# Regrouping the backward attention loop: where a group's sums, transpositions, query gradient and job matmuls stand, and which engines copy and add

## The chip, the cores and the metric

The kernel runs on one core of a Trainium2 chip. Its engines work from queues of their own and meet at semaphores: TensorE (PE, with its weight loads as PEld), VectorE (DVE), ScalarE (ACT), GpSimd (POOL) and SyncE (SP). SP here only issues DMAs, GpSimd issues DMAs and does a little arithmetic. Matmul results go to PSUM, everything else lies in SBUF. The metric is the device time of the one core in microseconds.

## The reference

The program computes a transformer block of attention and a gated feed-forward part that both read the same normalised input, and then the gradients of that sum by an output gradient. There are 2048 tokens, a model width of 448, 16 heads of 28 and a hidden width of 1792.

```
x  = A_x
xn = layernorm(x)
q, k, v = split(xn @ wqkv)                     # 16 heads of 28
p  = softmax(q @ k.T * 28 ** -0.5)
A  = (p @ v) @ wo
B  = (silu(xn @ w_gate) * (xn @ w_up)) @ w_down
out = x + A + B
grads of out by x, wqkv, wo, w_gate, w_up, w_down, for a given grad_out
```

Outputs are out and the six gradients, all in bf16. In the backward pass of attention, p is computed again from q and k. With dp = dO @ v.T (less its row sums), ds = p * dp; then dv = p.T @ dO, dk = ds.T @ q and dq = ds @ k, the last two times the scale.

## The kernel before

The program has three stages. The first (to about 690 us in the profile) normalises, projects, runs the forward attention and, between its steps, the feed-forward part with its weight gradients. The second is the backward attention, from about 694 to 1503 us; the change lies in it alone. The third adds up the gradient of x.

**Units and groups.** The backward loop (line 944) goes over 512 units. A unit is one pair of heads, one block of 512 keys (kc) and one tile of 128 queries (qi within a half w of the sequence). Eight units with the same pair, key block and half are a group, so there are 64 groups; W is the number of the group and pos the place of step k in it (k = 8 W + pos). Two groups cover all 16 query tiles of a key block; eight groups cover a pair.

**A unit.** TensorE computes the scores s of unit k (line 957, two matmuls, one per head, in two row strips of the array) and dp of unit k - 1 (line 967, in the other two strips). ScalarE takes E = exp(s) (line 976). VectorE multiplies dp by E into ds (line 984); ds tiles hold two units. The row sums and the softmax denominators are folded into spare columns of the operands, so that this one product gives ds.

**PSUM.** s, dp and the output of the transpositions share three buffers "sd" of two banks each, taken in turn: the s of a unit normally takes the buffer whose ds product was three units ago, and the dp the buffer of the E just computed. One bank, "aux", is shared by the query gradient and the jobs, one after the other. One bank, "acc", holds the sums for keys and values.

**A group's other work** is placed by hand at positions of the loop, on TensorE in the order of the program:
- acc_mm (line 857): the sums of E times dO and ds times q, four matmuls a unit, in four column strips. Three units at position 3 and five at position 6.
- The query gradient needs ds transposed, tile dsT. Units 0 to 5 of a group are transposed by three DMAs from the SP queue (line 986), each of two units (512 KB). Units 6 and 7 are transposed on TensorE by pe_transpose (line 887) at position 2 of the next group, 16 matmuls against the identity; the two halves are copied out by ScalarE and VectorE (line 895).
- dq_mm (line 897): the query gradient of the group before, 16 matmuls, one half at position 4 and one at position 5. dq_out (line 911): at position 6 VectorE scales the result out of PSUM and adds it to an fp32 tile dq_acc over the four key blocks; at the fourth it writes a bf16 tile, which an SP transposition and two GpSimd DMAs take away one step later.
- A job: a piece of other work that needs TensorE, one for nearly every group (list at lines 729 to 733): 16 rows of the block's output (y, 19 matmuls), 2 x 16 rows of the gradient that comes back through the feed-forward weights (dx, 14 or 15 matmuls), and 14 pieces of the gradient of wqkv (dwq, 64 small matmuls). A job's matmuls are dealt out in thirds over position 7 of the group before and positions 0 and 1; job_out (line 834) at position 2 is ScalarE's copy out of PSUM and a DMA from GpSimd. The job of group W is loaded two groups ahead (job_load, line 735).

**Buffers.** E has eight buffers, ds five of two units, dsT two. The loop runs eight steps past the last unit.

**Order of the queues.** The kernel is scheduled by hand: each engine executes in program order. In a step that is: SP loads; scores; dp; job_out and dq_out; exp; ds; the DMA transposition of ds; DMAs put off from earlier steps (sp_later); job matmuls; pe_transpose; acc_mm; dq_mm.

Of the kernel before, what the change touches and what calls it, by code (L numbers as in the profile page):

```python
# [25 lines left out]
P = 128  # L26
# [3 lines left out]
SCALE = DH ** -0.5  # L30
# [8 lines left out]
def kernel(  # L39
# [19 lines left out]
    pe, act, dve, pool, sp = nc.tensor, nc.scalar, nc.vector, nc.gpsimd, nc.sync  # L59
# [46 lines left out]
    op1 = bst.enter_context(tc.tile_pool(name="op1", bufs=1))  # L106
# [38 lines left out]
    for b in range(1, 4):  # L145
# [9 lines left out]
        out=r_ones[:], in_=ident_f[:].rearrange("p (a b) -> p a b", b=HP)[:, :, 28:30],  # L155
# [529 lines left out]
    ast = ExitStack()  # L685
    ckp = ast.enter_context(tc.tile_pool(name="ckp", bufs=3))
    spg_.append(ast.enter_context(tc.tile_pool(name="spg", bufs=2)))
    ework = ast.enter_context(tc.tile_pool(name="ework", bufs=8))
    dwork = ast.enter_context(tc.tile_pool(name="dwork", bufs=5))
    twin = ast.enter_context(tc.tile_pool(name="twin", bufs=2))  # L690
    dqa = ast.enter_context(tc.tile_pool(name="dqa", bufs=1))
    ps_acc = ast.enter_context(tc.tile_pool(name="ps_acc", bufs=1, space=PSUM))

    UW = 8
# [116 lines left out]
    def job_mms(i, ps):  # L811
        j = jobs[i]
        if j[0] == "dwq6":
            return dwq_half_mms(0, j[1], ps, True, 0) + dwq_half_mms(0, j[1] + 1, ps, False, 192)
        if j[0] == "dwq":
            return dwq_mms(j[1], j[2], ps)
        if j[0] == "y":
            t, x = chunk[i]
            out = []
            for n in range(NFC + G):  # L820
                rhs = (wtile["wd"][:, n, :] if n < NFC else wo_pad[:, n - NFC, :D])
                out.append(lambda n=n, rhs=rhs: pe.matmul(ps[:, :D], lhsT=t[:, n, :], rhs=rhs,  # L822
                                                          start=(n == 0), stop=False))
            out.append(lambda: pe.matmul(ps[:, :D], lhsT=ident_bf[:], rhs=x[:], start=False, stop=True))
            return out
        t, x = chunk[i]
        w = wtile[("wg", "wu")[j[1]]]
        out = [lambda n=n: pe.matmul(ps[:, :D], lhsT=t[:, n, :], rhs=w[:, n, :],  # L828
                                     start=(n == 0), stop=(n == NFC - 1 and x is None)) for n in range(NFC)]
# [57 lines left out]
    def pe_transpose(W):  # L887

        ds, dsT = DS[W * 4 + 3], st[("dsT", W)]
        ps = ps_sd.tile([P, 2, 8, P], BF16, name="sd")  # L890
        for u in range(2):
            for i in range(8):
                pe.transpose(ps[:, u, i, :], ds[:, u, i // 4, (i % 4) * P:(i % 4 + 1) * P], ident_bf[:])  # L893
        for u, eng in enumerate((act.copy, dve.tensor_copy)):
            eng(out=dsT[:, 6 + u].rearrange("p j c q -> p (j c) q"), in_=ps[:, u])  # L895

    def dq_mm(W, half):
        pr, kc, w, _ = units[W * UW]
# [13 lines left out]
    def dq_out(W):  # L912
        pr, kc, w, _ = units[W * UW]
        g, hp = pr // 2, pr % 2
        ps = st["dq"]
        if (pr, w) not in dqacc:
            dqacc[(pr, w)] = dqa.tile([P, 512], FP32, name=f"dq_acc{w}")
        acc = dqacc[(pr, w)]
        if kc == 0:
            dve.tensor_scalar(out=acc[:], in0=ps[:], scalar1=SCALE, scalar2=None, op0=ALU.mult)  # L920
            return
        if kc < 3:
            dve.scalar_tensor_tensor(out=acc[:], in0=ps[:], scalar=SCALE, in1=acc[:], op0=ALU.mult, op1=ALU.add)
            return
        o = outp.tile([P, 512], BF16, name="dq_o")
        dve.scalar_tensor_tensor(out=o[:], in0=ps[:], scalar=SCALE, in1=acc[:], op0=ALU.mult, op1=ALU.add)
        dq = dsp[pr][1]

        def later():
            sp.dma_start_transpose(out=dq[:, w].rearrange("p c s r -> p c (s r)"), in_=o[:])  # L930
            for s_ in range(2):
                k0 = 4 * w + 2 * s_
                pool.dma_start(
                    out=dqkv_d[k0:k0 + 2, 64 * hp:64 * hp + 64, g, :].rearrange("k p s -> p k s"),
                    in_=o[64 * s_:64 * s_ + 64, :].rearrange("p (k s) -> p k s", k=2))
        sp_later.append((k_now[0] + 1, later))
# [4 lines left out]
    job_load(1)  # L941
    job_load(2)
    fillers = []
    for k in range(N + UW):
        W, pos = k // UW, k % UW
        k_now[0] = k
        if k < N:
            pr, kc, w, qi = units[k]
            if pos == 0:
                job_load(W + 2)  # L950
            if pos == 4:
                extra_load(W)
            q, kv = qd[pr]
            qt = 8 * w + qi
            s_ps = ps_sd.tile([P, 2, 512], FP32, name="sd")
            for j in range(2):
                pe.matmul(s_ps[:, j, :], lhsT=q[HP * j:HP * j + HP, qt * P:(qt + 1) * P],  # L957
                          rhs=kv[HP * j:HP * j + HP, kc * 512:(kc + 1) * 512],
                          start=True, stop=True, tile_position=(HP * j, 0))
        if 1 <= k <= N:  # L960
            pr, kc, w, qi = units[k - 1]
            q, kv = qd[pr]
            qt = 8 * w + qi
            d_ps = ps_sd.tile([P, 2, 512], FP32, name="sd")
            for j in range(2):
                r = 64 + HP * j
                pe.matmul(d_ps[:, j, :], lhsT=q[r:r + HP, qt * P:(qt + 1) * P],  # L967
                          rhs=kv[r:r + HP, kc * 512:(kc + 1) * 512],
                          start=True, stop=True, tile_position=(r, 0))
        if pos == 2 and W in jobs:  # L970
            job_out(W, st["job"])
        if pos == 6 and W >= 1:
            dq_out(W - 1)
        if k < N:
            E[k] = ework.tile([P, 2, 512], BF16, name="E")
            act.activation(out=E[k][:], in_=s_ps[:], func=ACT.Exp, scale=SCALE)  # L976
        if 1 <= k <= N:
            u = k - 1
            if qi == 0:
                st[("dsT", u // UW)] = twin.tile([P, UW, 2, 4, P], BF16, name="dsT")  # L980
            if u % 2 == 0:
                DS[u // 2] = dwork.tile([P, 2, 2, 512], BF16, name="ds")
            ds = DS[u // 2]
            dve.tensor_tensor(out=ds[:, u % 2], in0=d_ps[:], in1=E[u][:], op=ALU.mult)  # L984
            if qi in (1, 3, 5):
                sp.dma_start_transpose(
                    out=st[("dsT", u // UW)][:, qi - 1:qi + 1].rearrange("p u j c q -> p (u j c) q"),
                    in_=ds[:].rearrange("p u j c -> p (u j c)"))
        while sp_later and sp_later[0][0] <= k:
            sp_later.pop(0)[1]()  # L990

        if pos == 7 and W + 1 in jobs:
            st["job"] = ps_x.tile([P, 512], FP32, name="aux")
            fillers = job_mms(W + 1, st["job"])
        if pos in (7, 0, 1):
            n = -(-len(fillers) // (3 - (pos + 1) % UW))
            for f in fillers[:n]:
                f()
            fillers = fillers[n:]
        if pos == 2 and W >= 1:  # L1000
            pe_transpose(W - 1)
        if pos == 3:
            for u in range(max(k - 6, 0), k - 3):
                acc_mm(u)
        if pos in (4, 5) and W >= 1:
            dq_mm(W - 1, pos - 4)
        if pos == 6:
            for u in range(k - 6, min(k - 1, N)):
                acc_mm(u)
    while sp_later:  # L1010
        sp_later.pop(0)[1]()
    ast.close()
# [110 lines left out]
```

## Time and profile before

| | us |
|---|---|
| Median of 3 runs (lowest, highest) | 1583.67 (1571.13, 1587.04) |
| The profiled execution | 1572.41 |
| Its span, first to last instruction | 1570.6 |
| TensorE busy, matmuls | 1447.8 |
| VectorE busy | 1123.3 |
| ScalarE busy | 1171.0 |
| GpSimd busy | 231.4 |
| First and last ds product of the backward loop | 694.2, 1503.0 |
| First matmul of the last stage | 1516.4 |

The profile is one execution. Its page gives the busy time of each engine, the span in 40 slices, the chain of work that ended last, and the costliest groups of instructions by source line, with what ended the idle time before them. The trace behind it can be asked for the waits between engines, for a timeline of one engine in a stretch of time, and for busy times and the granted TensorE clock of a stretch. In timeline rows the columns are start, length, engine, line, operation, tile written and tiles read, shapes, count, and in square brackets the idle time before and what ended it. A busy engine need not be at its peak: matmuls overlap, and four that lie in different strips of the array run side by side.

### The profile page before, as it was taken

To read this page: it belongs to the slowest core of one execution; us is meant where nothing else is said; L and a number is where in the kernel's file an instruction comes from. 1 tells how busy PE (TensorE), PEld (TensorE's weight loads), DVE (VectorE), ACT (ScalarE), POOL (GpSimd) and SP (SyncE) were. 2 spreads that over 40 slices of the span, in tenths; PEclk is the share of its full clock that TensorE was granted. 3 is DMA by queue.
4 is the path that set the end of the run, shared out by engine and by line. 5 is a ranking of instruction groups with operands and counts; after the bars stand their busy time and mean duration, and the time that the engine had idled before them with its cause. 6 is when DMAs were issued, how large, how long until landed. Compare 5 with 4: busy or idle time off the path is not lost.

```text
span 1570.6 us, 31535 instructions
## 1 busy us (share of the span) xinstructions
PE 1447.8 (92%) x12278; PEld 592.2 (38%) x12278; DVE 1123.3 (72%) x1459; ACT 1171.0 (75%) x1312; POOL 231.4 (15%) x431
## 2 busy tenths in 40 slices
PE   6889999999999999969989999899899899998968
PEld 3233333333333333323333344333335334533424
DVE  7465656665666666538878888788888888998835
ACT  4578888888888877637767777677777788887824
POOL 4001111111111111110111111101102111110212
PEclk7799999999999999979999999999999999999979
DMA  5566647776767778579999999999999999999974
GB/s 160 114 147 139 145 102 162 144 150 127 157 140 154 139 152 171 129 189 210 227 219 232 220 164 201 202 206 222 205 185 202 210 229 193 198 204 202 166 221 134
DMA packets 764854, 277.69 MB, mean 177 GB/s; under 512 B 730960, under 2 KB 744208, under 8 KB 764704
## 3 DMA queue, kind: packets, MB, share of 16 engines
q1 hardware_dynamic: 748944, 238.90, 77.9%
q0 software_dynamic: 14960, 36.60, 8.5%
q8 instruction: 96, 1.57, 0.4%
q14 instruction: 54, 0.44, 0.1%
q10 hardware_dynamic: 800, 0.17, 0.1%
HBM read 64.15 MB, written 59.24 MB: 79 GB/s over the span
## 4 chain that ended last, share of the span: by engine, by line
PE 72%; DMA 11%; DVE 7%; ACT 6%; issue 2%; SPq 1%; DVEq 0%; ACTq 0%; POOL 0%
PE s_ps L651 9%; PE f_ps L413 8%; DMA dsT<-ds 8%; PE f_ps L439 8%; PE sd L957 7%; PE aux L828 6%; PE acc L867 5%; PE o_ps L628 5%; PE aux L822 4%; PE aux L908 3%; PE sd L967 3%; PE f_ps L198 3%; ACT E L976 3%; ACT dsT L895 3%; PE sd L1039 2%; PE sd L893 2%
## 5 line engine op out<-in xcount | busy, mean ns | idle before, releaser
L984 DVE TENSOR_TENSOR ds<-sd,E 128x1024 bf16<-128x1024 f32 x512 | 610.5, 1219 | 91.7 <-PE sd L967 40.6
L976 ACT ACTIVATE E<-sd 128x1024 bf16<-128x1024 f32 x512 | 522.4, 1027 | 202.1 <-PE sd L967 142.8
L655 ACT ACTIVATE eT<-s_ps 128x1024 bf16<-128x1024 f32 x512 | 496.5, 1021 | 137.7 <-PE s_ps L651 136.7
L957 PE MATMUL sd<-KV,QD 32*128 32x512 bf16 x1024 | 203.7, 392 | 37.1 <-DVE dsT L895 18.7
L967 PE MATMUL sd<-KV,QD 32*128 32x512 bf16 x1024 | 204.9, 391 | 9.5 <-ACT E L976 7.5
L651 PE MATMUL s_ps<-qT,kT 32*128 32x512 bf16 x1024 | 196.9, 392 | 0.5 <-ACT eT L655 0.5
L957 PEld LDWEIGHTS <-QD 32*128 32x128 bf16 x1024 | 61.0, 91 | 216.1 <-issue 204.5
L867 PE MATMUL acc<-E,dOsp 128*32 128x512 bf16 x1024 | 141.5, 400 | 0.2 <-DMA ck<-hO_d 0.2
L867 PE MATMUL acc<-ds,Qsp 128*32 128x512 bf16 x1024 | 141.5, 401 | 0.0
L439 PE MATMUL f_ps<-xnT,wgu 128*128 128x512 bf16 x448 | 119.3, 384 | 9.0 <-DVE w_sb L465 9.0
L908 PE MATMUL aux<-dsT,Ksp 128*32 128x512 bf16 x1024 | 92.7, 402 | 28.3 <-DMA dsT<-ds 28.2
L651 PEld LDWEIGHTS <-kT 32*128 32x128 bf16 x1024 | 47.4, 91 | 162.0 <-issue 158.2
L628 PE MATMUL o_ps<-eT,v_sp 128*32 128x512 bf16 x1024 | 104.0, 399 | 4.3 <-DMA v_sp<-vT 4.1
L828 PE MATMUL aux<-W,ck 128*128 128x448 bf16 x448 | 101.6, 355 | 0.0
L413 PE MATMUL f_ps<-xn_sp,f_sp 128*128 128x448 bf16 x448 | 98.9, 354 | 0.0
L967 PEld LDWEIGHTS <-QD 32*128 32x128 bf16 x1024 | 76.9, 91 | 58.5 <-issue 45.0
L413 PEld LDWEIGHTS <-f_sp 128*128 128x128 bf16 x672 | 58.9, 98 | 66.9 <-issue 20.4
L895 DVE COPY dsT<-sd 128x1024 bf16<-128x1024 bf16 x64 | 44.2, 691 | 50.9 <-ACT dsT L895 50.9
L893 PE MATMUL sd<-ident_bf,ds 128*128 128x128 bf16 x1024 | 69.3, 221 | 2.5 <-DVE ds L984 1.7
L451 DVE SCALAR_TENSOR_TENSOR g<-t_sb,f_ps 128x512 f32<-128x512 f32 x56 | 38.4, 685 | 44.0 <-ACT t_sb L449 44.0
L895 ACT COPY dsT<-sd 128x1024 bf16<-128x1024 bf16 x64 | 64.9, 1014 | 6.5 <-PE sd L893 3.9
L893 PEld LDWEIGHTS <-ds 128*128 128x128 bf16 x1024 | 59.2, 99 | 17.3 <-issue 14.5
(145 smaller groups left out, 1695.5 us busy)
## 6 DMA issues: line engine op xcount, KB each, us to landing
ck<-hO_d SPq DMA_DIRECT2D x17, 576.0 KB, 4.8
hO_d<-hduT SPq DMA_DIRECT2D x56, 128.0 KB, 3.4
da_d<-hduT SPq DMA_DIRECT2D x56, 128.0 KB, 3.0
du_d<-hduT SPq DMA_DIRECT2D x56, 128.0 KB, 3.3
ck<-da_d SPq DMA_DIRECT2D x16, 448.0 KB, 4.2
ck<-du_d SPq DMA_DIRECT2D x16, 448.0 KB, 4.1
dq_c<-dqkv_d SPq DMA_DIRECT2D x8, 768.0 KB, 5.4
dqkv_d<-dkv_o POOLq DMA_DIRECT2D x64, 64.0 KB, 4.5
```

The costliest lines, as they stand in the source:

```text
L413: pe.matmul(acc[:, :D], lhsT=src[:, t, wi, :], rhs=rhs[:, t, :D], start=(t == 0), stop=(t == NT - 1))
L439: pe.matmul(st[name][:], lhsT=w(c), rhs=src[:, tsl, c, :], start=(c == 0), stop=(c == 3))
L628: pe.matmul(o_ps[HP * hh:HP * (hh + 1), :], lhsT=v[:, kt, HP * hh:HP * (hh + 1)], rhs=e[hh // 2][:, hh % 2, :], start=(kt == 0), stop=(kt ...
L651: pe.matmul(s_ps[:, j, :], lhsT=kT[r:r + HP, kt * P:(kt + 1) * P], rhs=qT[r:r + HP, qc * 512:(qc + 1) * 512], start=True, stop=True, tile_ ...
L655: act.activation(out=e[:], in_=s_ps[:], func=ACT.Exp, scale=SCALE)
L828: out = [lambda n=n: pe.matmul(ps[:, :D], lhsT=t[:, n, :], rhs=w[:, n, :], start=(n == 0), stop=(n == NFC - 1 and x is None)) for n in ran ...
L867: pe.matmul(acc[r:r + HP, :], lhsT=src[:, qt, 64 * hp + HP * j:64 * hp + HP * j + HP], rhs=m[:, j, :], start=(qt == 0), stop=(qt == NT - 1 ...
L893: pe.transpose(ps[:, u, i, :], ds[:, u, i // 4, (i % 4) * P:(i % 4 + 1) * P], ident_bf[:])
L957: pe.matmul(s_ps[:, j, :], lhsT=q[HP * j:HP * j + HP, qt * P:(qt + 1) * P], rhs=kv[HP * j:HP * j + HP, kc * 512:(kc + 1) * 512], start=Tru ...
L967: pe.matmul(d_ps[:, j, :], lhsT=q[r:r + HP, qt * P:(qt + 1) * P], rhs=kv[r:r + HP, kc * 512:(kc + 1) * 512], start=True, stop=True, tile_p ...
L976: act.activation(out=E[k][:], in_=s_ps[:], func=ACT.Exp, scale=SCALE)
L984: dve.tensor_tensor(out=ds[:, u % 2], in0=d_ps[:], in1=E[u][:], op=ALU.mult)
```

## The change

The group's work gets other positions, and two steps other engines.

- The sums: five units of the group before at position 0, the other three at position 3.
- pe_transpose of the group before at position 1 (was 2), and both copies out of PSUM by VectorE.
- The query gradient, both halves at position 2, of the group two back (was: of the group before, at 4 and 5). Its dq_out is at position 3.
- dq_out: ScalarE scales the result out of PSUM into fp32, and GpSimd adds it to dq_acc; the bf16 result comes from GpSimd's add too. A new pool dqs has two buffers for that.
- A job's matmuls are dealt out over positions 3 to 7 of its own group; job_out is at position 0 of the next.
- The DMA transposition of ds, and the claim of the dsT buffer with it, stand at the end of a step, after TensorE's work.
- E gets nine buffers. The loop runs twelve steps past the last unit, for the query gradients of the last two groups.

```diff
-    ework = ast.enter_context(tc.tile_pool(name="ework", bufs=8))
+    ework = ast.enter_context(tc.tile_pool(name="ework", bufs=9))
+    dqs = ast.enter_context(tc.tile_pool(name="dqs", bufs=2))
...
-        for u, eng in enumerate((act.copy, dve.tensor_copy)):
-            eng(out=dsT[:, 6 + u].rearrange("p j c q -> p (j c) q"), in_=ps[:, u])
+        for u in range(2):
+            dve.tensor_copy(out=dsT[:, 6 + u].rearrange("p j c q -> p (j c) q"), in_=ps[:, u])
...
+        d = acc if kc == 0 else dqs.tile([P, 512], FP32, name="dq_s")
+        act.activation(out=d[:], in_=ps[:], func=ACT.Copy, scale=SCALE)
         if kc == 0:
-            dve.tensor_scalar(out=acc[:], in0=ps[:], scalar1=SCALE, scalar2=None, op0=ALU.mult)
             return
         if kc < 3:
-            dve.scalar_tensor_tensor(out=acc[:], in0=ps[:], scalar=SCALE, in1=acc[:], op0=ALU.mult, op1=ALU.add)
+            pool.tensor_tensor(out=acc[:], in0=acc[:], in1=d[:], op=ALU.add)
             return
         o = outp.tile([P, 512], BF16, name="dq_o")
-        dve.scalar_tensor_tensor(out=o[:], in0=ps[:], scalar=SCALE, in1=acc[:], op0=ALU.mult, op1=ALU.add)
+        pool.tensor_tensor(out=o[:], in0=acc[:], in1=d[:], op=ALU.add)
...
-    for k in range(N + UW):
+    for k in range(N + UW + 4):
...
-        if pos == 2 and W in jobs:
-            job_out(W, st["job"])
-        if pos == 6 and W >= 1:
-            dq_out(W - 1)
+        if pos == 0 and W - 1 in jobs:
+            job_out(W - 1, st["job"])
+        if pos == 3 and W >= 2:
+            dq_out(W - 2)
...
+        if pos == 0 and 1 <= W <= NW:
+            for u in range(k - 8, k - 3):
+                acc_mm(u)
+        if pos == 1 and 1 <= W <= NW:
+            pe_transpose(W - 1)
+        if pos == 2 and W >= 2:
+            dq_mm(W - 2, 0)
+            dq_mm(W - 2, 1)
+        if pos == 3 and 1 <= W <= NW:
+            for u in range(k - 6, k - 3):
+                acc_mm(u)
+        if pos == 3 and W in jobs:
             st["job"] = ps_x.tile([P, 512], FP32, name="aux")
-            fillers = job_mms(W + 1, st["job"])
-        if pos in (7, 0, 1):
-            n = -(-len(fillers) // (3 - (pos + 1) % UW))
+            fillers = job_mms(W, st["job"])
+        if pos >= 3:
+            n = -(-len(fillers) // (8 - pos))
...
-        if pos == 2 and W >= 1:
-            pe_transpose(W - 1)
-        if pos == 3:
-            for u in range(max(k - 6, 0), k - 3):
-                acc_mm(u)
-        if pos in (4, 5) and W >= 1:
-            dq_mm(W - 1, pos - 4)
-        if pos == 6:
-            for u in range(k - 6, min(k - 1, N)):
-                acc_mm(u)
+        if 1 <= k <= N and qi in (1, 3, 5):
+            Wd = (k - 1) // UW
+            if qi == 1:
+                st[("dsT", Wd)] = twin.tile([P, UW, 2, 4, P], BF16, name="dsT")
+            sp.dma_start_transpose(
+                out=st[("dsT", Wd)][:, qi - 1:qi + 1].rearrange("p u j c q -> p (u j c) q"),
+                in_=ds[:].rearrange("p u j c -> p (u j c)"))
```

More of the change, by code (lines that the diff above doesn't have):

```diff
@@ L978 @@
             u = k - 1
-            if qi == 0:
-                st[("dsT", u // UW)] = twin.tile([P, UW, 2, 4, P], BF16, name="dsT")
             if u % 2 == 0:
@@ L984 @@
             dve.tensor_tensor(out=ds[:, u % 2], in0=d_ps[:], in1=E[u][:], op=ALU.mult)
[L985 to L988, printed above, removed]
         while sp_later and sp_later[0][0] <= k:
             sp_later.pop(0)[1]()
-        if pos == 7 and W + 1 in jobs:
+        if pos == 0 and 1 <= W <= NW:
[10 more added lines that the diff above has]
+        if pos == 3 and W in jobs:
             st["job"] = ps_x.tile([P, 512], FP32, name="aux")
-            fillers = job_mms(W + 1, st["job"])
-        if pos in (7, 0, 1):
-            n = -(-len(fillers) // (3 - (pos + 1) % UW))
+            fillers = job_mms(W, st["job"])
+        if pos >= 3:
+            n = -(-len(fillers) // (8 - pos))
             for f in fillers[:n]:
```

## The prediction

> **What bounds the kernel now.** Read the page first (busy shares, costliest groups), then the waits of the backward stage (700 to 1500 us), then the timelines of two of its groups of eight units. TensorE is 92% busy, so the change is judged by what TensorE and the pair VectorE/ScalarE do within one group, not by a sum over the kernel.
>
> ```profile
> PE 1447.8 (92%) x12278; PEld 592.2 (38%) x12278; DVE 1123.3 (72%) x1459; ACT 1171.0 (75%) x1312; POOL 231.4 (15%) x431
> ...
> L984 DVE TENSOR_TENSOR ds<-sd,E 128x1024 bf16<-128x1024 f32 x512 | 610.5, 1219 | 91.7 <-PE sd L967 40.6
> ...
> L895 DVE COPY dsT<-sd 128x1024 bf16<-128x1024 bf16 x64 | 44.2, 691 | 50.9 <-ACT dsT L895 50.9
> ...
> L895 ACT COPY dsT<-sd 128x1024 bf16<-128x1024 bf16 x64 | 64.9, 1014 | 6.5 <-PE sd L893 3.9
> ```
>
> The reader is to see that per group VectorE does eight ds products of 1.22 us, a copy of 0.69 and a dq sum of 0.68, and that its copy waits 0.8 us each time for ScalarE's copy. The waits of the stage (us in total, times, longest):
>
> ```profile
> DVE dsT L895 <- ACT dsT L895: 48.9, 63, 1.8
> ...
> PE aux L908 <- DMA dsT<-ds: 28.2, 20, 3.0
> ...
> PE sd L957 <- DVE dsT L895: 18.7, 61, 0.4
> ```
>
> In 20 groups of 64 the query gradient waits for the DMA transposition of ds. One such group on TensorE (start, length, idle before):
>
> ```profile
> 1006.93 0.39 PE L908 MATMUL aux<-dsT,Ksp 128*32 128x512 bf16 x2
> 1009.14 0.67 PE L908 MATMUL aux<-dsT,Ksp 128*32 128x512 bf16 x6 [1.82 <-DMA dsT<-ds]
> 1009.75 0.61 PE L957 MATMUL sd<-KV,QD 32*128 32x512 bf16 x2
> ```
>
> After the idle 1.8 us the matmuls take 0.61 instead of 0.39 us, for some 4 us. And the job thirds of an undisturbed group on TensorE:
>
> ```profile
> 1279.30 0.39 PE L957 MATMUL sd<-KV,QD 32*128 32x512 bf16 x2
> 1279.31 0.39 PE L967 MATMUL sd<-KV,QD 32*128 32x512 bf16 x2
> 1279.63 1.12 PE L828 MATMUL aux<-W,ck 128*128 128x448 bf16 x5
> 1280.68 0.39 PE L957 MATMUL sd<-KV,QD 32*128 32x512 bf16 x2
> 1280.81 0.39 PE L967 MATMUL sd<-KV,QD 32*128 32x512 bf16 x2
> ...
> 1282.19 0.39 PE L967 MATMUL sd<-KV,QD 32*128 32x512 bf16 x2
> ```
>
> ScalarE's exp of the same two units:
>
> ```profile
> 1279.73 1.02 ACT L976 ACTIVATE E<-sd 128x1024 bf16<-128x1024 f32 x1 [0.76 <-PE sd L967]
> 1281.11 1.02 ACT L976 ACTIVATE E<-sd 128x1024 bf16<-128x1024 f32 x1 [0.36 <-PE sd L957]
> ```
>
> Two units take 2.88 us here, 1.44 each: five job matmuls (1.05) and the score pairs (0.32) fill TensorE. From the starts of the transposition (L893) in TensorE's timeline, the 63 steps from group to group between 709.5 and 1503.1 sum to 793.6 us. An undisturbed one lasts 12.29 with an out job (15 of them), 11.75 with any other. 15 x 12.29 + 48 x 11.75 = 748.4; so **45.2 us are lost to the transposition waits**, 28.2 idle and the rest matmuls at half clock (in the group from 1003.53 the granted clock averages 0.89, in that from 1272.26 it is 1.00).
>
> **Part by part.** Rules taken from the undisturbed group: scores s to exp start 0.43; exp 1.02, then d 0.06 later (it takes that buffer); d to ds start 0.53; ds 1.22, one after another every 1.14; copy 0.69, every 0.60; pair s and d together 0.33 on TensorE; five units of sums 1.20, so three 0.76; 16 transpositions 1.03; half a query gradient 0.55 to 0.61, so both 0.97; job matmuls 0.187 each and 0.11 for the switch.
>
> *Query gradient two groups on.* The last DMA transposition of a group leaves after unit 5 and lands after 5.6 us (median; 8.9 at most). It has now over a group more. That removes 45.2 us. Nothing in the rows is late next: the SP queue waits for VectorE's products (406.7 us) more than for anything else, so it is not behind. The first transposition of a group now waits, with SP's queue behind it (job loads, row loads), for the query gradient that frees its dsT buffer; by the table below this ends at 4.9 and the products at 5.9, so it costs nothing.
>
> *Inside a group.* Copies on VectorE: two of 0.69 in a row, in place of 0.75 waiting and 0.69: no change there; ScalarE loses 1.01. The dq sum leaves VectorE (-0.68, so -0.60 in a row) for ScalarE: an eviction of 128x512 to fp32, between 0.53 (row_o, 448 wide) and 0.69 (dkv_o, 512 wide); I take 0.69, nearest in size and place. VectorE's floor is then 8 x 1.14 + 2 x 0.60 = 10.3 us a group. Followed in order (times from position 0's scores, dx job of 14 matmuls):
> - 0: s 0, d 0.23, sums of five until 1.75. ScalarE evicts the job 0.20-0.73, exp until 1.65; ds of unit 7 0.87-2.09.
> - 1: s 1.75, d 1.76; transpositions need that ds: 2.15-3.18. ds 2.29-3.51, copies 3.43 to 4.72.
> - 2: s 3.26 (exp ends 3.20), d 3.57 (ds ends 3.51), query gradient 3.89-4.86; exp 3.69-4.71; ds 4.63-5.85.
> - 3: s 4.86, d 4.87, sums 5.2-5.95; dq eviction 5.0-5.7, so the job finds its bank free at 5.95; three job matmuls until 6.62; exp 5.6-6.6; ds 5.8-7.0.
> - 4 to 7: three job matmuls each (two in the last) take 0.67, with the pair 1.0, so d waits for exp and ds sets the pace: d at 6.66, 8.13, 9.16, 10.63; next s at 11.43.
>
> So **11.45 us instead of 11.75**; by the same steps 11.6 with 15 job matmuls (d x 1) and 12.0 instead of 12.29 with 19. The weight jobs (64 small matmuls, 24 in 1.13 us) count as 11.5; the group without a job as 10.8; group 1, without a query gradient, 11.4. From position 0 of group 1 to that of group 64: 11.4 + 15 x 12.0 + 10.8 + 30 x 11.5 + 16 x 11.6 = 732.8, where the trace has 1501.34 - 706.04 = 795.3: **-62.5**, of which 45.2 are the waits and 17 the tighter group. Bounds of the group: VectorE's floor 10.3, which would need every exp and score on time (63 x 1.15 = 72 us more; I give it no chance, half of it a small one); no gain, 11.75.
>
> *GpSimd adds.* 48 of 128x512. Nearest row: the last stage's add of 128x448, 1033 ns, so 1.18. GpSimd's queue has four DMA issues of 0.6 and is 15% busy; its dq stores and the SP transposition of dq (two groups in eight) wait 1.2 longer, with the last dsT of the group behind, which has its spare group. Costs nothing unless the add holds VectorE up (rival 2). The Trainium skill (SBUF — State Buffer, Who interferes with whom) says that GpSimd and VectorE exclude each other when VectorE has two SBUF inputs or a two-port mode. Here ds and both copies read PSUM, so by that rule nothing is held, and the sum stays; another of its pages (Perfetto Trace Analysis, Optimizing Scalar/DVE Operations) warns that moving work between these two engines might not help, which would be rival 2.
>
> *Start.* Group 0 loses its sums at position 6 (700.28 to 702.97 at half clock): units run at ds pace, group 1 begins near 701.5 instead of 706.04. TensorE then warms up later; I take -3 of 0 to -4.5.
>
> *End.* Sums of five, transpositions and the query gradients of two groups now follow the last unit. Before, 9.35 us pass from the last s (1501.34) to the first load of the last stage (1510.69). After: transpositions to 3.3, gradient 62 to 4.2, its eviction to 5.3, add to 6.5, four DMA issues on GpSimd to 8.9, second add to 10.1, SP's transposition 1.2: 11.3 to 12. I take +2.5, of 0 to +8.
>
> *ework 9, dqs 2.* One more buffer each: cost nothing in SBUF time; no wait on E appears in the rows.
>
> **Sum.** 1570.6 - 62.5 - 3 + 2.5 = 1507.6 span; the profiled execution took 1572.41, 1.8 more: **1510**. The runs shown have median 1583.67, 11 above this execution, and reach 1587.04; part of that spread may be the same waits.
>
> **Rivals.**
> 1. *The group does not tighten*, only the waits go: the transpositions stand one position nearer to the ds they read (0.06 us to spare in my table), and any lag is paid by TensorE, in order. At 11.75 and 12.29 the sum gives 1572.4 - 45.2 - 0.5 = 1527.
> 2. *The add holds VectorE.* 48 x 1.18 = 57 us, if every add stops it for its length and nothing hides it: 1510 + 57 = 1567, no change. For it: VectorE is the pace; against: in the last stage the VectorE op at 1527.17 that reads PSUM and SBUF takes 0.62 beside GpSimd's add as elsewhere.
> 3. *Slower: ds of unit 7 late.* If VectorE is a whole unit behind at position 1, transpositions wait 1.22 us in each group, copies and the score buffer follow: 11.45 + 1.25 = 12.7, 63 x 1.25 = 79 us: 1589. It decides from 1.0 us a group on (63 us, all of the gain). Against: VectorE idles 0.2 us before ds of unit 0 in the table.
> 4. *DMA is the limit.* The DMA share is 1.07 in an undisturbed group and 1.27 (290 GB/s) while transpositions run alone; 208 of 290 GB/s leaves room down to 8.4 us a group. If it held at 11.75, 1527 again.
>
> **Chances.** Forecast (1485 to 1520) 0.47; rivals 1 and 4 (1520 to 1545) 0.25; better than the forecast (VectorE's idle 1.1 us a group halved, 32 us: 1478) 0.08; rival 2 0.11; rival 3 0.09. The range takes in all but rival 3 and the far end of "better": 1478 to 1570; the forecast's own is 1485 to 1520. Within 1% is about what a measurement of this kernel can tell from no change. Faster by over 1% is the first three, 0.80; within 1% rival 2, 0.11; slower rival 3, 0.09.
>
> **What would show it.** Right: no wait of the query gradient for DMA dsT; steps between transpositions of 11.4 to 11.6 (12.0 with an out job); two VectorE copies back to back; granted clock 1.00 through the stage; VectorE idle some 1.1 us in a dx group. Wrong: an idle before the transpositions above 0.3 us that ends with ds; ds products over 1.22 us beside adds; a job's first matmul waiting for ScalarE's dq eviction; a last stage that starts over 10 us later after the last scores than before.

## The result, and where the time went

The changed kernel takes 1567.2 us (median of 20 runs, 1558.0 to 1573.1), the kernel before 1574.97 beside it (20 runs); the ratio is 0.9935, 95% interval 0.9912 to 0.9957. So it gains 0.65%, some 8 to 10 us, where 62 were forecast. Ratios leave out runs more than 1.5% above the fastest of the same kernel, and so can differ from the quotient of two medians. The profiled execution took 1558.67 us, span 1556.9.

Four lines of the changed kernel's page (engine busy times; then line, engine, operation, busy and mean duration, idle time before and what ended most of it):

```profile
PE 1428.1 (92%) x12278; PEld 577.4 (37%) x12278; DVE 1121.8 (72%) x1459; ACT 1148.4 (74%) x1312; POOL 293.3 (19%) x479
...
L984 DVE TENSOR_TENSOR ds<-sd,E 128x1024 bf16<-128x1024 f32 x512 | 607.8, 1220 | 121.7 <-DMA dsT<-ds 48.0
...
L896 DVE COPY dsT<-sd 128x1024 bf16<-128x1024 bf16 x128 | 82.1, 683 | 3.7 <-PE sd L894 3.5
...
L925 POOL TENSOR_TENSOR dq_acc<-dq_acc,dq_s 128x512 f32<-128x512 f32 x32 | 40.5, 1265 | 130.5 <-ACT dq_s L921 130.5
```

The two copies no longer wait for ScalarE (3.7 us idle in all, 50.9 before), the ds product keeps its 1.22 us. But the largest idle time ahead of that product, 48.0 us, now ends with the DMA transposition; before the change that product never waited for it. The waits of the backward stage (700 to 1500 us; total, times, longest):

```profile
DVE ds L984 <- DMA dsT<-ds: 48.0, 35, 3.6
...
PE sd L959 <- DVE ds L984: 31.7, 38, 2.7
...
PE aux L909 <- DMA dsT<-ds: 4.8, 2, 3.4
```

The query gradient's wait is gone as forecast (28.2 us before, 4.8 now, in two waits at the very end). In its place VectorE waits: a ds product overwrites one of five ds buffers, and the DMA transposition that reads that buffer's former content, of the group before, has not landed. VectorE's product is what the score buffers, TensorE's transposition and the next group wait for, so this wait is paid by all.

Undisturbed groups run as the prediction's table had them. TensorE's transpositions (start, length), first over one step with such a wait, then over two without:

```profile
1120.05 1.05 PE L894 MATMUL sd<-ident_bf,ds 128*128 128x128 bf16 x16 [0.73 <-DVE ds L984]
1134.98 1.07 PE L894 MATMUL sd<-ident_bf,ds 128*128 128x128 bf16 x16
...
1322.53 1.07 PE L894 MATMUL sd<-ident_bf,ds 128*128 128x128 bf16 x16
1334.00 1.05 PE L894 MATMUL sd<-ident_bf,ds 128*128 128x128 bf16 x16
1345.40 1.05 PE L894 MATMUL sd<-ident_bf,ds 128*128 128x128 bf16 x16
```

The first step lasts 14.93 us, the other two 11.47 and 11.40 (the table said 11.45). With an out job it is 11.97 (12.0 forecast). The 63 steps from the first transposition to the last:

| | undisturbed step, dx / out job | 15 and 48 of them | the 63 steps | excess |
|---|---|---|---|---|
| before | 11.75 / 12.29 | 748.4 | 793.6 | 45.2 |
| after | 11.45 / 11.97 | 729.2 | 780.9 | 51.7 |

The tighter group gave its 19.2 us, and 6.5 of them went into an excess that did not vanish but grew. The first transposition comes 6.1 us earlier (703.45 against 709.51); 2.3 of these lie ahead of the loop's first product (691.94 against 694.24), before anything that was changed, and part of the rest comes from the transposition standing one position earlier in the group. The end takes back the same 6.1: from the start of the last transposition to the first matmul of the last stage 13.2 us before, 19.3 now. Together -12.7 - 6.1 + 6.1, and 1.0 less in the last stage: the 13.7 by which the two spans differ.

Where is the excess? In both kernels mostly between about 776 and 1300 us (50.0 of the 51.7 us after, 37.6 of the 45.2 before), in the same stretches: there a group issues a job load and, besides, a piece of the next head pair, of rows or of weights. SP's queue of the changed kernel there (start, length, queue, line; one row can hold several transfers):

```profile
1112.72 3.15 SPq L1011 DMA_TRANSPOSE dsT<-ds  x1
1115.96 0.53 SPq L748 DMA_DIRECT2D ck<-da_d  x1
1116.60 3.78 SPq L1011 DMA_TRANSPOSE dsT<-ds  x1
1120.44 0.58 SPq L599 DMA_DIRECT2D QD<-qT_d  x1
1121.11 1.22 SPq L932 DMA_TRANSPOSE dq_sp<-dq_o  x1
1122.42 6.62 SPq L1011 DMA_TRANSPOSE dsT<-ds  x2
1129.13 0.54 SPq L748 DMA_DIRECT2D ck<-da_d  x1
```

And VectorE beside it:

```profile
1111.40 1.22 DVE L984 TENSOR_TENSOR ds<-sd,E 128x1024 bf16<-128x1024 f32 x1 [0.20 <-PE sd L969]
...
1124.85 1.23 DVE L984 TENSOR_TENSOR ds<-sd,E 128x1024 bf16<-128x1024 f32 x1 [0.15 <-ACT dkv_o L874]
1129.06 2.36 DVE L984 TENSOR_TENSOR ds<-sd,E 128x1024 bf16<-128x1024 f32 x2 [2.99 <-DMA dsT<-ds]
```

The product that ends at 1112.62 is transposed from 1122.42 on, so the queue is ten microseconds late, and VectorE stands still for 2.99 us ahead of 1129.06. In the kernel before, the queue was late too. These are SP's rows ahead of the waiting query gradient that the prediction shows (it goes on at 1009.14), then the second of the two transpositions at 997.24 as a narrower window shows it, and the product that it reads:

```profile
992.37 0.53 SPq L747 DMA_DIRECT2D ck<-da_d  x1
992.99 3.54 SPq L986 DMA_TRANSPOSE dsT<-ds  x1
996.58 0.57 SPq L607 DMA_DIRECT2D dOsp<-spo_d  x1
997.24 9.60 SPq L986 DMA_TRANSPOSE dsT<-ds  x2
1006.89 1.27 SPq L930 DMA_TRANSPOSE dq_sp<-dq_o  x1
...
1003.53 3.30 SPq L986 DMA_TRANSPOSE dsT<-ds  x1
...
996.58 1.21 DVE L984 TENSOR_TENSOR ds<-sd,E 128x1024 bf16<-128x1024 f32 x1
```

The product ends at 997.79, and its transposition begins at 1003.53, 5.7 us later: the transposition ahead of it, issued behind a load of rows, holds the queue until then. It lands at 1009.10, 5.6 us after its issue, no more than the median. So the transposition was not slow to land, it was issued late.

How late the queue is, from the end of a product to the start of the row that transposes it (mean, and the most):

| | 776 to 900, 980 to 1135, 1180 to 1300 us | 730 to 775, 1311 to 1402 us (undisturbed) |
|---|---|---|
| before | 2.6, 6.6 | 1.1, 3.8 |
| after | 7.0, 11.9 | 3.1, 6.1 |

This could have been read before the forecast, but not from the sum of SP's waits. That view counts waits for products in the late stretches as everywhere else; between 980 and 1135 us, before the change:

```profile
SPq L986 <- DVE ds L984: 86.9, 34, 4.8
```

SP's rows leave 6.0 us of that stretch open, and 64.2 us of the whole stage (700 to 1500). So most of the 406.7 us that the view adds up over the stage is not time in which the queue stood idle: none of the 192 rows begins before its product has ended, and the view counts up to the last product that ended before the row did. Rows without gaps are no sign either: in the changed kernel they fill 96% of the late stretches, and 96% of the undisturbed one from 1311 to 1402.

The chain of work through the stage (700 to 1500 us), before and after:

```profile
by line: DMA dsT<-ds 15.8%; PE sd L957 14.3%; PE aux L828 11.3%; PE acc L867 10.5%; PE aux L822 7.0%; PE aux L908 6.8%; PE sd L967 6.6%; ACT E L976 5.2%; ACT dsT L895 5.2%; PE sd L893 4.1%; DVE dsT L895 3.5%; DVE ds L984 2.4%; issue 2.2%; P
```

```profile
by line: DMA dsT<-ds 22.7%; PE sd L959 11.6%; PE acc L868 10.7%; ACT E L978 9.3%; DVE ds L984 6.8%; PE aux L909 6.8%; PE sd L969 6.6%; issue 6.0%; PE sd L894 5.3%; PE aux L823 4.6%; PE aux L829 3.5%; PE aux L765 1.9%; PE aux L767 0.8%; DVE 
```

The transposition was the largest item already; after the change it is 22.7%.

### The profile page after: what moved, and what is told of

Its sections match the earlier page's. It is cut to its first block, busy times and chain, and to the rows that moved or that the text cites. A ratio compares the mean times of both kernels' runs of the same rounds, so it can differ in the third digit from the quotient of the medians.

```text
span 1556.9 us, 31518 instructions
## 1 busy us (share of the span) xinstructions
PE 1428.1 (92%) x12278; PEld 577.4 (37%) x12278; DVE 1121.8 (72%) x1459; ACT 1148.4 (74%) x1312; POOL 293.3 (19%) x479
## 3 DMA queue, kind: packets, MB, share of 16 engines
q1 hardware_dynamic: 748944, 238.90, 79.8%
## 4 chain that ended last, share of the span: by engine, by line
PE 65%; DMA 15%; DVE 9%; ACT 6%; issue 4%; SPq 1%; DVEq 0%; POOL 0%; ACTq 0%; POOLq 0%
DMA dsT<-ds 12%; PE s_ps L651 9%; PE f_ps L413 8%; PE f_ps L439 8%; PE sd L959 6%; PE acc L868 5%; ACT E L978 5%; PE o_ps L628 5%; DVE ds L984 4%; PE aux L909 3%; PE sd L969 3%; PE sd L894 3%; PE f_ps L198 3%; PE sd L1043 2%; PE aux L823 2%
## 5 line engine op out<-in xcount | busy, mean ns | idle before, releaser
L984 DVE TENSOR_TENSOR ds<-sd,E 128x1024 bf16<-128x1024 f32 x512 | 607.8, 1220 | 121.7 <-DMA dsT<-ds 48.0
L969 PE MATMUL sd<-KV,QD 32*128 32x512 bf16 x1024 | 203.7, 390 | 12.9 <-ACT E L978 4.6
L959 PEld LDWEIGHTS <-QD 32*128 32x128 bf16 x1024 | 57.6, 91 | 208.2 <-issue 194.5
L829 PE MATMUL aux<-W,ck 128*128 128x448 bf16 x448 | 112.5, 356 | 0.0
L969 PEld LDWEIGHTS <-QD 32*128 32x128 bf16 x1024 | 69.1, 91 | 64.1 <-issue 60.3
L894 PE MATMUL sd<-ident_bf,ds 128*128 128x128 bf16 x1024 | 70.8, 224 | 15.7 <-DVE ds L984 15.5
L896 DVE COPY dsT<-sd 128x1024 bf16<-128x1024 bf16 x128 | 82.1, 683 | 3.7 <-PE sd L894 3.5
L909 PE MATMUL aux<-dsT,Ksp 128*32 128x512 bf16 x1024 | 71.8, 400 | 4.8 <-DMA dsT<-ds 4.8
L894 PEld LDWEIGHTS <-ds 128*128 128x128 bf16 x1024 | 62.4, 100 | 30.5 <-issue 30.4
L925 POOL TENSOR_TENSOR dq_acc<-dq_acc,dq_s 128x512 f32<-128x512 f32 x32 | 40.5, 1265 | 130.5 <-ACT dq_s L921 130.5
```

Source lines behind the costliest of these rows:

```text
L909: pe.matmul(ps[r:r + HP, :], lhsT=Ks[:, kc * 4 + kt, 64 * hp + HP * j:64 * hp + HP * j + HP], rhs=dsT[:, 4 * s_:4 * s_ + 4, j, kt, :], sta ...
```

## The experiments

The theory after reading the traces, Q: in a group with a job load and an extra load (the piece of a head pair, of rows or of weights), the transfers on SP's queue last longer than the group; the lag adds up over such groups, and wherever the first consumer of the transpositions stands (query gradient before, ds buffer now) it pays. Its forms: what counts is issue time on SP (S) or bytes in the DMA engines (D). Rivals: five ds buffers are too few for the transposition's own 5.7 us, whatever else is loaded (B); and the prediction's own reading, that the distance of the query gradient was the fault.

All ratios are to the kernel before, measured beside it on the same chip. "Steps" are the 63 steps as above, "excess" their sum less the undisturbed ones.

**Loads from another queue.** In both kernels all plain loads of the backward loop are issued by GpSimd, only transpositions stay on SP (ldq[0] is SP up to the loop, GpSimd from there):

```diff
...
-            sp.dma_start(out=t[:], in_=hO_d[j[1]])
+            ldq[0].dma_start(out=t[:], in_=hO_d[j[1]])
...
+    ldq[0] = pool
...
```

> The changed kernel with the plain loads inside the backward loop (job tiles, head pairs, weights, rows of dO) issued from GpSimd's queue instead of SP's; the DMA transpositions stay on SP. Theory S (where loads fall into a group, the time that SP's queue needs to issue its DMAs, some 3.1 us for each transposition of ds, exceeds the group, so the products wait for their buffers): SP is relieved of 1 to 2 us a group, the 48 us of products waiting for the transposition and the 5 us of the query gradient go, ratio to the kernel before near 0.963. Theory D (the DMA engines are full in those stretches; bytes decide): nothing changes, ratio 0.99. Theory B (only the five ds buffers are too few for the transposition's landing time): nothing changes, 0.99.

> The kernel before with the same loads on GpSimd's queue. S: the 28 us of query gradient waiting for the transposition go and the half clock after them, 45 us in all, ratio near 0.971, and the change then is worth some 20 us (19 by the shorter group). D: ratio 1.00. B: 1.00, since nothing waits for a ds buffer before.

Changed kernel 1.0164 (1.007 to 1.0258), kernel before 1.0461 (1.0389 to 1.0533): slower, against every expectation. Undisturbed steps stay at 11.40 to 11.47, the disturbed ones reach 26.7; excess 83.7 us. SP's queue of the changed kernel with these loads:

```profile
1009.08 1.27 SPq L882 DMA_TRANSPOSE dkv_sp<-dkv_o  x1
1010.45 29.57 SPq L1013 DMA_TRANSPOSE dsT<-ds  x5
1040.13 1.77 SPq L933 DMA_TRANSPOSE dq_sp<-dq_o  x1
```

Five transpositions take 29.57 us on a queue that carries nothing else, while GpSimd's queue issues rows at 1009.84, a job load at 1014.70 and weights at 1022.97. Busy times, clock, DMA share and GB/s of eight microseconds there, and of the changed kernel as it is at the same time of its own trace, where it is not at the same unit:

```profile
1017.00:1025.00 8.00, 5.82 (x66) 2.69 (x66) 4.96 (x6) 5.15 (x6) 3.25 (x5) 1.00 1.23 86
```

```profile
1017.00:1025.00 8.00, 5.83 (x74) 2.78 (x73) 6.82 (x8) 4.55 (x6) 0.58 (x1) 1.00 1.11 234
```

There the DMA engines are busier (1.23 against 1.11) and move a third as much (86 against 234 GB/s). Over the whole 29.57 us the difference is smaller: 141 GB/s at a share of 1.14, against 208 at 1.13. So S fell, as far as it says that SP's issue order is the only bound: the transfers share something behind the queues. The run changes two things at once, though: on the page the loads pass to another kind of queue (software_dynamic 78.8 MB in place of 36.6), and whether it is that kind or the overlap that costs was not separated. The Trainium skill (DMA: Bandwidth & Descriptors, Issuing engines are not separate DMA queues) says that transfers issued by several engines run on the same 16 DMA engines and that a second issuer saves only sequencer time. The trace agrees so far as the transpositions get longer while SP's queue carries nothing else; what the second issuer saves is here far less than what it costs.

**A sixth ds buffer**, paid for with one job tile less (job loads then come one group ahead, not two):

```diff
-    ckp = ast.enter_context(tc.tile_pool(name="ckp", bufs=3))
+    ckp = ast.enter_context(tc.tile_pool(name="ckp", bufs=2))
...
-    dwork = ast.enter_context(tc.tile_pool(name="dwork", bufs=5))
+    dwork = ast.enter_context(tc.tile_pool(name="dwork", bufs=6))
...
-                job_load(W + 2)
+                job_load(W + 1 if W else 0)
```

> The changed kernel with six ds buffers instead of five; to make room a job's tile is loaded one group ahead into two buffers instead of two groups ahead into three. S: one more buffer of two units covers 2.9 us of lag once in a stretch of several heavy groups, so 5 to 20 us are gained, ratio 0.981 to 0.990. D: as S. B: most of the 48 us go, ratio near 0.967.

> Both together. S: as the loads on GpSimd alone, within 5 us, near 0.962. D: as the six buffers alone, 0.981 to 0.990. B: as the six buffers alone, 0.967.

0.9958 (0.9921 to 0.9995): no gain. The products' wait for the transposition falls from 48.0 to 29.0 us, the query gradient's rises from 4.8 to 8.6 with 9.1 of its weight loads, and the steps are 776.0, excess 46.8. With the loads on GpSimd's queue as well: 1.005 (1.0007 to 1.0093), excess 76.7; its ten runs lie between 1572.04 and 1622.45 us, with a median of 1601.65. B fell: a buffer more defers the wait, and the queue is no less late (a transposition of ds begins 7.4 us after its product in the median of the whole loop, 5.2 in the changed kernel).

**The extra loads left out.** Every group computes with the first head pair, the first rows and the first weights, and the two loads of the gradient's rows stand ahead of the loop; job loads stay:

```diff
     def extra_load(W):
 
+        return
         pr, r = W // 8, W % 8
...
```

> The changed kernel with the extra loads of the backward groups left out (head pairs 1 to 7, rows of groups 1 to 3, weights; every group computes with the first pair, the first rows and the first weight, the gradient's rows are loaded ahead of the loop; the products are not the reference's). Theory Q (in groups with an extra load SP's queue of transpositions and loads carries more than a group lasts, so ds products wait for the transposition that frees their buffer; the groups between are undisturbed): steps between transpositions are 11.45 and 11.97 nearly throughout, the 51.7 us of excess shrink below 15, time near 1527, ratio to before 0.97. Theory B (five ds buffers are too few for the transposition's own 5.7 us whatever else is loaded): excess stays, ratio 0.99.

> The kernel before with the same extra loads left out. Theory Q: the waits of its query gradient for the transposition vanish too, without any change of order; steps 11.75 and 12.29, excess of 45.2 us below 12, ratio 0.975. Theory of the prediction (the transposition's latency against the distance of the query gradient): the waits stay near 28 us and the ratio at 0.99 or above.

Changed kernel 0.9637 (0.9604 to 0.967), 1516.96 us; kernel before 0.9803 (0.9774 to 0.9832), 1542.71. In the changed kernel the steps are 736.3, excess 7.1; 52 of 63 are within 0.1 of 11.42 or 11.97, and the median lateness falls from 5.2 to 2.5 us. In the kernel before the steps are 758.6, excess 10.2, and the transposition waits that the change was to remove are nearly gone without it (waits of its query gradient, 28.2 before):

```profile
PE aux L909 <- DMA dsT<-ds: 6.4, 5, 1.9
```

Between these two, that is without the disturbance, the change is worth 1542.71 - 1516.96 = 25.8 us. The distance alone was not the fault; B falls a second time, for with five buffers and no extra loads the products wait 10.8 us in all, and the chain of the stage (700 to 1440 us) has the transposition at 6.9% in place of 22.7:

```profile
by line: ACT E L988 17.1%; PE sd L969 15.3%; PE acc L869 13.8%; PE sd L979 10.2%; PE aux L910 7.7%; DMA dsT<-ds 6.9%; PE aux L824 6.8%; PE aux L830 6.4%; issue 4.3%; PE sd L895 4.0%; PE aux L766 2.3%; ACT dkv_o L875 1.3%; DVE ds L994 1.1%; 
```

**As many issues, few bytes.** The same left out, but at each place a transfer of 16 columns (128 for the row transpositions):

```diff
...
+            sp.dma_start(out=nxt(16), in_=wT_d[0][:, 0, :16])
...
```

> As the first of these, but with as many issues on SP's queue at the same places, each of a few columns only (16 columns, 128 for the two transpositions of rows); computed as in the first. If bytes in the DMA engines are what disturbs a group (D): as without extra loads, 0.97. If it is the number of issues on the queue (S): the disturbed groups stay disturbed, 0.985 to 0.99.

0.971 (0.9668 to 0.9752); steps 744.9, excess 15.7. Of the 44.6 us of steps that leaving the loads out saves, 36.0 are saved although every issue is still there. So some four fifths belong to the bytes (D), one fifth to the issues. With the bytes go two thirds of these loads' DMA packets (the page counts 748944 of the kind hardware_dynamic for the changed kernel, 737712 here and 732208 with the loads left out), so bytes and packets are not told apart.

**The job loads left out instead.** Each job computes with the first job's tile (78 loads fewer in the loop: 47 tiles and 31 rows; the expectation counts 81), the extra loads stay:

```diff
+        if i > 1 and j[0] in ("y", "dx"):
+            chunk[i] = (chunk[1][0], chunk[1][1] if j[0] == "y" or j[1] == 1 else None)
+            return
```

> The changed kernel with the job loads left out instead (48 of 448 or 576 KB, 33 of 112 KB; each job computes with the first job's tile; extra loads stay). Theory Q, any load counts alike: 81 loads fewer, the queue has room in nearly every group, excess below 15 us, ratio 0.97. If only the extra loads matter: excess stays near 45, ratio 0.99.

0.9633 (0.9601 to 0.9665); steps 729.8, excess 0.6, median lateness 1.1 us. The extra loads do no harm by themselves. It is the sum of job loads, extra loads and three transpositions a group that is too much, and taking away either kind ends it.

**One part undone, the dq sum back on VectorE:**

```diff
-        act.activation(out=d[:], in_=ps[:], func=ACT.Copy, scale=SCALE)
...
-            pool.tensor_tensor(out=acc[:], in0=acc[:], in1=d[:], op=ALU.add)
+            dve.scalar_tensor_tensor(out=acc[:], in0=ps[:], scalar=SCALE, in1=acc[:], op0=ALU.mult, op1=ALU.add)
```

> The changed kernel with one part undone: the dq sums are made by VectorE out of PSUM as before, not by ScalarE and GpSimd. By the prediction's table VectorE's sum of 0.68 us then stands between the products of units 2 and 3 and pushes what follows by up to 0.6: undisturbed steps 11.8 to 12.0 in place of 11.45 (12.3 to 12.5 in place of 11.97). Of 63 x 0.45 = 28 us part is taken back where the queue is behind: time 1575 to 1595, ratio 1.00 to 1.013. Theory Q alone, with the sum hidden: steps 11.45, ratio 0.993.

**One part undone, a copy back on ScalarE:**

```diff
-        for u in range(2):
-            dve.tensor_copy(out=dsT[:, 6 + u].rearrange("p j c q -> p (j c) q"), in_=ps[:, u])
+        for u, eng in enumerate((act.copy, dve.tensor_copy)):
+            eng(out=dsT[:, 6 + u].rearrange("p j c q -> p (j c) q"), in_=ps[:, u])
```

> The changed kernel with one part undone: the first of the two copies of the TensorE transposition is made by ScalarE again (1.01 us there, 0.68 less on VectorE). By the table ScalarE's exp of unit 2 of the group then comes about 0.5 us later: undisturbed steps 11.7 to 11.95 in place of 11.45, time 1570 to 1590. If ScalarE has the room (it idles 1.5 us a group): steps 11.45 or less, time as the changed kernel, 0.99.

Undisturbed transpositions of the two, the dq sum first (start, length):

```profile
1334.55 1.05 PE L894 MATMUL sd<-ident_bf,ds 128*128 128x128 bf16 x16
1346.53 1.05 PE L894 MATMUL sd<-ident_bf,ds 128*128 128x128 bf16 x16
```

```profile
1347.42 1.05 PE L894 MATMUL sd<-ident_bf,ds 128*128 128x128 bf16 x16
1359.21 1.05 PE L894 MATMUL sd<-ident_bf,ds 128*128 128x128 bf16 x16
```

| | undisturbed step, dx / out job | 15 and 48 of them | the 63 steps | excess | ratio |
|---|---|---|---|---|---|
| before | 11.75 / 12.29 | 748.4 | 793.6 | 45.2 | 1 |
| dq sum on VectorE | 11.95 / 12.50 | 761.1 | 784.4 | 23.3 | 0.995 (0.9916 to 0.9985) |
| a copy on ScalarE | 11.78 / 12.27 | 749.5 | 784.6 | 35.1 | 0.9932 (0.9905 to 0.9958) |
| the whole change | 11.45 / 11.97 | 729.2 | 780.9 | 51.7 | 0.9935 (0.9912 to 0.9957) |

The group steps are as the table of the prediction had them (11.8 to 12.0 and 11.7 to 11.95 were expected), so each part does tighten the group; the time expected of both, slower than the change, failed. A group looser by 0.33 to 0.5 us costs 20 to 32 us in undisturbed steps and nothing in the end, for the excess shrinks by nearly as much. The second of these also tells what the rest of the change is worth at the kernel before's own group step: 793.6 - 784.6 = 9 us.

**Extra loads in other groups.** Same transfers, but groups without a job load take two or three, and 23 groups have both kinds (37 by a count in the changed kernel, not 45 as the expectation says):

```diff
-        if 1 <= r <= 4 and pr + 1 < NPR:
-            load_pair(pr + 1, [r - 1])
...
+    for p_, at_ in ((1, (1, 2, 3, 4)), (2, (8, 10, 12, 14)), (3, (17, 18, 19, 20)), (4, (24, 26, 28, 30)),
+                    (5, (34, 36, 37, 38)), (6, (40, 42, 44, 46)), (7, (49, 50, 51, 52))):
...
```

> The changed kernel with the same extra loads in other groups: in the groups that issue no job load (15 to 19, 36 to 39, 48 to 51, 60 to 62) two or three of them, so that only 23 groups carry a job load and an extra load together, in place of some 45; between the pieces of a head pair a group without one; rows of the gradient with nothing behind them. Same bytes, same number of issues, same results. Theory Q (a group is disturbed when its own loads and transpositions take SP's queue longer than the group lasts, and the five ds buffers let little of it be made up): the excess of 51.7 us falls to 20 to 35, ratio to before 0.972 to 0.983. If only the total of bytes counts (a bound of the DMA over the whole stage): as the changed kernel, 0.993.

> The changed kernel with the extra loads placed a second time, after what the first placing showed: one piece of rows came too late for the sums there (5.8 us of TensorE), and two large pieces in a group without a job load still disturbed it. Now the two transpositions of rows have light groups (no job load) nearly to themselves, the row piece that came late comes five groups earlier, the gate weights lie between the pieces of head pairs in the first 14 groups, which are longer (11.97). Same bytes, issues and results. Theory Q: the first stretch to group 16 stays at 11.97, no wait of the sums for rows, excess 25 to 38 us against the 42.5 of the first placing, ratio to before 0.978 to 0.986. If only the total of bytes counts: no better than the first placing, 0.987 or above.

The first placing takes 1550.39 us, 0.987 (0.9835 to 0.9904): the best version here that computes everything, by the two ratios some 10 us better than the change alone, though the intervals nearly touch. Its steps 2 to 14 are undisturbed (11.96 to 11.98) where the change has 15.79 among them. The excess is still 42.5, not 20 to 35: groups 15 to 19, without a job load but with two large pieces, take up to 13.8 us, and one row piece came too late for TensorE:

```profile
1292.75 0.61 PE L873 MATMUL acc<-E,dOsp 128*32 128x512 bf16 x2 [5.82 <-DMA dOsp<-spo_d]
```

The second placing mends that wait and is no better: 0.9888 (0.9838 to 0.9939), steps 778.2, excess 49.0; now steps 6 to 14 are disturbed again (up to 15.17), where the pieces of pairs have weights and rows between them. Counted from the two plans, 28 groups of the second placing have both kinds of load, against 23 of the first and 37 of the changed kernel, and the excess follows that order (49.0, 42.5, 51.7). The same bytes placed otherwise win back at most 9.2 us of it. So where the loads stand matters a little; that the rest is set by the bytes of the whole stage would fit, but no run shows it.

## Why the prediction was wrong

- **The group's table was right.** 11.45 and 12.0 forecast, 11.45 and 11.97 measured; undone parts moved it as the same table says. Without the extra loads the kernel took 1516.96 us, beside the 1510 forecast: the forecast comes near to the changed kernel without the disturbance.
- **The step that failed** is the removal of 45.2 us, in its sentence "Nothing in the rows is late next: the SP queue waits for VectorE's products (406.7 us) more than for anything else, so it is not behind." Most of the 406.7 us is not idle time: SP's rows leave 64.2 us of the stage open. And the queue was behind: in the stretches where the waits were, a transposition began 2.6 us after its product on the mean and up to 6.6, in the prediction's own example 5.7. The waits were put down to the distance between the transposition and the query gradient, a latency, while they came from transfers that queued up. A consumer moved away from a late queue stops waiting; the queue stays late, and the next thing that it holds, the ds buffer, takes the wait: 28.2 us became 4.8, and a wait of 48.0 appeared on VectorE.
- **The new wait of SP for the query gradient** that frees the dsT tile, which the prediction put at nothing, does cost nothing: in all groups from the third on the gradient has ended 0.1 to 1.0 us before the product that the group's first transposition reads (the table: 1.0).
- **Rival 1** had it the wrong way round: the group tightened and the waits stayed.
- **Rival 4 named the mechanism and was priced wrongly.** "208 of 290 GB/s leaves room down to 8.4 us a group" takes every byte at the rate that transpositions reach alone. But the rate does not tell the groups apart: the changed kernel moves 212 to 213 GB/s in the three late stretches (776 to 900, 980 to 1135, 1180 to 1300 us), 225 between 730 and 775 us and 200 between 1311 and 1402, both undisturbed. No room can be read from it. Leaving out 78 job loads saves 51 us of steps (780.9 - 729.8), at least 0.6 us each, and 50 extra loads 44.6, some 0.9 each. The rival also was to hold all groups at 11.75; it holds mainly those with both kinds of load and those that follow, and leaves most others at 11.45. The mean step within the late stretches is 13.2 (12.9 before).
- **The tighter group** was worth the 17 us that were forecast for it (19.2 in steps), and nearly all of it is lost again: where the queue sets the pace, a faster group only makes it later (3.1 us in place of 1.1 even in the undisturbed stretches).
- **GpSimd's add** takes 1.265 us, not 1.18, and costs nothing: the products beside it keep 1220 ns. Rival 2 fell; that its 1567 us is what was measured is coincidence. The rule of the Trainium skill (SBUF — State Buffer, Who interferes with whom), by which a VectorE instruction with at most one input in SBUF, outside the two-port modes, does not contend with GpSimd, agrees with that.
- **Rival 3**, the product of unit 7 late for TensorE's transposition: 15.5 us in 23 places, none over 0.74 us, not 79. Such a wait of over 0.3 us was one of the prediction's signs of being wrong; 22 of the 23 lie in the late part, between 780 and 1300 us.
- **The start**, forecast as 3 us earlier, came 6.1 earlier by the first transposition, of which 3.8 fall within the loop.
- **The end** cost 7.0 us by the prediction's own measure (from the last scores to the first load of the last stage 9.35 before, 16.37 now) for the 2.5 taken, inside the 0 to 8 given. It is again the queue: two loads of the gradient's rows stand among the last transpositions.

```profile
1481.37 0.68 SPq L728 DMA_DIRECT2D W<-in_grad_out_dram  x1
1482.10 7.96 SPq L1011 DMA_TRANSPOSE dsT<-ds  x2
```

TensorE's last query gradient waits for them, twice:

```profile
1490.39 0.61 PE L909 MATMUL aux<-dsT,Ksp 128*32 128x512 bf16 x2 [3.35 <-DMA dsT<-ds]
1492.41 1.89 PE L909 MATMUL aux<-dsT,Ksp 128*32 128x512 bf16 x14 [1.42 <-DMA dsT<-ds]
```

What stays open: what the transfers share. That it lies behind the queues, and depends more on what the transfers carry than on their number, is shown; whether the DMA engines' time, the SBUF side of a transposition or DRAM is the limit was not separated, nor bytes from packets.

## What to carry to other kernels

Before a consumer is moved away from a transfer that comes late, ask whether the transfer lands slowly or starts late: in the very stretch where the wait falls, compare the start of its row with the end of what it reads. If it starts late, the queue is behind, and the wait will go to the next buffer that the transfer holds. A stage's total of waits, a queue without gaps or a transfer rate can't tell that. And once a shared queue sets the pace, shortening the compute group buys little: first take transfers away, or spread them. Another queue is no way out by itself, as the loads on GpSimd's show.

## What was not expected of the hardware

- With the plain loads on GpSimd's queue, beside DMA transpositions on SP's, the transpositions slow down: five took 29.57 us, the longest landed 22.1 us after issue (9.7 at most in the changed kernel), and the DMA engines moved 141 GB/s in that time at a share of 1.14 (208 at 1.13 in the changed kernel).
- A DMA transposition's row on SP is longer behind a job load: in the changed kernel 3.6 us in the median of 44, against 2.8 behind another transposition of ds (55 rows).
- TensorE's granted clock falls after a wait of 2.46 us: it is 0.50 between 1131.40 and 1133.00, and matmuls that took 0.39 us take 0.61 to 0.64 from 1131.47 on. So a wait on VectorE costs more than its own length.
